# Three-piece weight conversion beside the second and third block pair, and a start with loads on two queues, in a fused attention and two-network kernel

## The chip, the cores and the metric

The kernel runs on one core of a Trainium2 chip. The metric is device time of one execution in microseconds (us). The engines are TensorE (PE, with its weight loads shown as PEld), VectorE (DVE), ScalarE (ACT), GpSimd (POOL) and SyncE (SP); SP computes nothing here, it issues DMAs. ACT issues DMAs too, in line with its arithmetic. "SPq" and "ACTq" in a profile row mark the issue of a DMA.

## The reference

```python
scores = scale * q_c @ k_c.T                # chunks of 64 tokens, 8 heads of 64, batch 8 x 576
attn = exp(scores - max); attn = attn / (sum + 1e-9)
x = (attn @ v_c)                            # 4608 tokens x 512, heads side by side
x = ((x @ moe_w_a) * (x @ moe_w_b)) @ moe_w_out                 # inner width 1536
out = (((x @ w1) * (x @ w2)) @ w3) @ w_out                      # inner width 1024
```

The weights arrive as 64-bit floats and q, k, v as 32-bit floats. The output is 4608 x 512 in 32 bits.

## The kernel before

**Tokens.** The 4608 tokens are nine blocks of 512. Blocks 0 and 1 are done first by plain products, blocks 2 to 7 in three pairs by a seven-product (Strassen) scheme, and block 8 alone; then the second network takes the same blocks. A product works on a high and a low part of each number, three 128x512 matrix instructions for one. One step of a network is one column of 128 inner features (`f`); the first network has 12 steps, the second 8. A pair starts with a burst (the output products of the pair before it) and goes on with its 12 steps.

**Beside the products.** Attention for later blocks is cut into pieces (`turn`, `scores`, `soft2`, `flip`, `apply`) in units of two heads of one block, and the conversion of weights into further pieces. A `Track` hands out pieces at marked points of a step, so that its share of the pieces is out when its share of the points has passed. All engines run what is written to them in the order of writing; nothing is moved at run time.

**Conversion.** The first network's weights are converted at the start, those of the second network beside the second and third pair: 40 tiles of 128x512. A tile is loaded by SP (512 KB, L173). Step one (`s1`) is a bit operation on VectorE (L179) and a rescaling on ScalarE (L180). Step two (`s2`) is three operations on VectorE (L185, L188, L189) and a sum on GpSimd (L195). The result is stored to HBM by ScalarE's queue (L157). `Pump` keeps the order. Its `run` first lets stores go that are due, then calls `begin`, which does `s1` for tiles up to two past the last finished one, then `s2` of the next tile. Beside the pairs a tile has two pieces, `run` and then a load, and there are three places for raw tiles, so the load of tile n+2 takes the place of tile n-1, whose store must have landed.

```python
            self.begin(self.done + 2)
            c, sink, eng = self.jobs[self.done]
            c.s2(eng)
...
            return [p for _ in range(n) for p in ((2.2, False, pump.run), (0.6, False, load))]
```

**Inside a step of a pair.** Four PSUM banks take the products (names `P`, L807). ScalarE copies three of them away (`c`, L892) and VectorE adds to those copies (L895) and multiplies (L922); a bank is free for a later product when its copy or sum is done. Then come pieces at the points, in the same queues.

**Start.** Units 0 to 3 (block 0) are loaded before all else: q, k, v of a unit in turn on SP, three weight tiles on ScalarE's queue. `ask` collects loads and `settle` writes them to a queue. q and k are turned by TensorE (L467) and copied by ScalarE with the tokens put back into order (L468); the softmax is scaled by VectorE (L370). A converted pair of weights gets its high part on ScalarE (L662) and its low part on VectorE (L658). Beside block 0's first three steps (`AHEAD`) run the units 4 to 7 of block 1 and three conversions a step, one in the first.

## Time and profile before

| | before |
|---|---|
| median of 3 runs | 1804.84 us (1803.17 to 1807.74) |
| the profiled execution's own time | 1824.92 us |
| its span, first to last instruction | 1823.1 us |
| mean granted TensorE clock | 0.948 of full |
| TensorE busy | 1625.3 us (89%) |
| VectorE, ScalarE, GpSimd busy | 888.3, 552.9, 449.7 us |

The profiled execution is one run with the hardware profiler on; it is 20.08 us (1.1%) longer than the median of the runs without it. Busy time is the time in which an engine has an instruction in work. A TensorE at clock 1.00 runs at 2.4 GHz, at half of that at 1.2 GHz. The stages of the span are: start and block 0's attention to 43.92 us, blocks 0 and 1 to 281.67, first pair to 517.60 (its steps from 331.85), second pair to 778.74 (steps from 560.28), third pair to 1050.69 (steps from 819.51), block 8 to 1254, second network to the end.

### The profile page before, as it was taken

To read this page: it belongs to the slowest core of one execution; us is meant where nothing else is said; L and a number is where in the kernel's file an instruction comes from. 1 tells how busy PE (TensorE), PEld (TensorE's weight loads), DVE (VectorE), ACT (ScalarE), POOL (GpSimd) and SP (SyncE) were. 2 spreads that over 40 slices of the span, in tenths; PEclk is the share of its full clock that TensorE was granted. 3 is DMA by queue.
4 is the path that set the end of the run, shared out by engine and by line. 5 is a ranking of instruction groups with operands and counts; after the bars stand their busy time and mean duration, and the time that the engine had idled before them with its cause. 6 is when DMAs were issued, how large, how long until landed. Compare 5 with 4: busy or idle time off the path is not lost.

```text
span 1823.1 us, 24483 instructions
## 1 busy us (share of the span) xinstructions
PE 1625.3 (89%) x8968; PEld 1289.9 (71%) x8968; DVE 888.3 (49%) x1460; ACT 552.9 (30%) x989; POOL 449.7 (25%) x350
## 2 busy tenths in 40 slices
PE   5789999889998887897887797999999999999998
PEld 3567777667776665675665676778877877878887
DVE  5658756565763554564455533345234252252231
ACT  4434434222242221242221242223132142242232
POOL 1223323111141221242232240001232231231232
PEclk8789999999999998998898898999999999999999
DMA  8658766776778677586775577878666666676685
GB/s 209 219 172 262 254 202 173 226 215 188 246 223 238 194 199 205 193 249 221 231 228 191 194 256 265 325 296 300 208 225 225 208 222 228 208 231 208 196 280 176
DMA packets 302071, 409.55 MB, mean 225 GB/s; under 512 B 176000, under 2 KB 196480, under 8 KB 301952
## 3 DMA queue, kind: packets, MB, share of 16 engines
q1 hardware_dynamic: 265568, 318.85, 57.9%
q10 hardware_dynamic: 36384, 89.14, 12.8%
q8 instruction: 71, 1.16, 0.3%
q14 instruction: 48, 0.39, 0.1%
HBM read 321.91 MB, written 85.98 MB: 224 GB/s over the span
## 4 chain that ended last, share of the span: by engine, by line
PE 40%; DMA 5%; DVE 2%; issue 2%; POOL 1%; ACT 1%; SPq 0%; ACTq 0%; POOLq 0%; DVEq 0%
PE P L807 22%; PE acc L836 12%; PE wf L1060 3%; DMA cv<-in_moe_w_dram 2%; PE pa0L L793 2%; PE pb0L L793 2%; DMA d<-cv 1%; DMA wo<-dwo 1%; DMA w<-dw 0%; DVE c L895 0%; PE w3p L1050 0%; ACT ev L845 0%; DMA su<-d 0%; DMA x2d<-ev 0%; POOL gl_5b L243 0%
## 5 line engine op out<-in xcount | busy, mean ns | idle before, releaser
L807 PE MATMUL P<-xP,w 128*128 128x512 f32 (+1 forms) x3192 | 777.0, 397 | 102.1 <-DVE c L895 51.2
L807 PEld LDWEIGHTS P<-xP,w 128*128 128x128 f32 x3192 | 597.2, 196 | 249.9 <-DVE c L895 60.8
L895 DVE TENSOR_TENSOR c<-P,c 128x512 f32<-128x512 f32 (+1 forms) x228 | 149.7, 660 | 341.4 <-PE P L807 332.6
L892 ACT COPY c<-P 128x512 f32<-128x512 f32 (+1 forms) x228 | 128.1, 564 | 229.2 <-PE P L807 219.8
L923 POOL TENSOR_TENSOR G<-c,c 128x512 f32<-128x512 f32 x68 | 88.5, 1302 | 416.5 <-DVE c L895 416.2
L242 ACT CAST gh<-c 128x512 fp32r<-128x512 f32 x68 | 42.2, 621 | 356.0 <-DVE c L922 342.1
L836 PE MATMUL acc<-gh,wo 128*128 128x512 f32 x384 | 145.1, 415 | 0.0
L243 POOL TENSOR_TENSOR gl<-c,gh 128x512 fp32r<-128x512 f32 x68 | 90.0, 1324 | 172.7 <-ACT gh L242 172.7
L836 PE MATMUL acc<-wo,gh 128*128 128x512 f32 x320 | 111.3, 391 | 0.5 <-ACT gh L242 0.5
L922 DVE TENSOR_TENSOR c<-P,c 128x512 f32<-128x512 f32 x68 | 46.9, 690 | 129.2 <-PE P L807 129.2
L836 PEld LDWEIGHTS acc<-gh,wo 128*128 128x128 f32 x384 | 76.5, 199 | 17.9
L195 POOL TENSOR_TENSOR cv<-cv 128x512 f32<-128x512 f32 x40 | 46.2, 1155 | 149.6 <-DVE cv L189 118.1
L793 PE MATMUL pa<-xq,w 128*128 128x512 f32 x288 | 78.0, 422 | 1.0 <-ACT xq L242 0.8
L836 PE MATMUL acc<-gl,wo 128*128 128x512 f32 x192 | 78.6, 409 | 0.0
L793 PE MATMUL pb<-xq,w 128*128 128x512 f32 x288 | 72.0, 400 | 0.8 <-DVE G0p L946 0.8
L845 ACT COPY ev<-acc 128x512 f32<-128x512 f32 x72 | 42.3, 588 | 95.2 <-PE acc L836 85.5
L836 PEld LDWEIGHTS acc<-wo,gh 128*128 128x128 f32 x320 | 60.1, 188 | 14.0 <-ACT gh L242 1.0
L793 PEld LDWEIGHTS pa<-xq,w 128*128 128x128 f32 x288 | 57.3, 204 | 14.9 <-ACT xq L242 1.6
L243 DVE TENSOR_TENSOR xP<-xP,xP 128x512 fp32r<-128x512 f32 (+1 forms) x56 | 46.7, 875 | 35.4 <-ACT xP L242 35.4
L836 PE MATMUL acc<-wo,gl 128*128 128x512 f32 x160 | 63.1, 394 | 0.8 <-POOL gl L243 0.8
L793 PEld LDWEIGHTS pb<-xq,w 128*128 128x128 f32 x288 | 54.5, 192 | 12.7 <-DVE G0p L946 1.2
L243 DVE TENSOR_TENSOR xP<-x,xP 128x512 fp32r<-128x512 f32 (+1 forms) x48 | 55.9, 1209 | 2.0 <-ACT xP L242 2.0
(149 smaller groups left out, 2291.8 us busy)
## 6 DMA issues: line engine op xcount, KB each, us to landing
w<-dw SPq DMA_DIRECT2D x228, 512.0 KB, 4.4
wo<-dwo SPq DMA_DIRECT2D x168, 512.0 KB, 4.6
dw<-w ACTq DMA_DIRECT2D x48, 512.0 KB, 5.2
w<-dw SPq DMA_DIRECT2D x92, 256.0 KB, 3.2
d<-cv ACTq DMA_DIRECT2D x40, 256.0 KB, 4.3
su<-d SPq DMA_DIRECT2D x20, 512.0 KB, 5.6
cv_o<-in_moe_w_out_dram SPq DMA_DIRECT2D x18, 512.0 KB, 5.3
x2d<-ev ACTq DMA_DIRECT2D x36, 256.0 KB, 4.7
```

Source lines behind the costliest of these rows:

```text
L195: eng.tensor_tensor(self.w, hi.bitcast(F32), lo, op=ALU.add)
L242: nc.scalar.copy(dst_h, src)
L243: eng_l.tensor_tensor(dst_l, src, dst_h, op=ALU.subtract)
L793: nc.tensor.matmul(ps, w[m][:, kk // 2, wp, kk % 2], xq[kk // 2][:, kk % 2, xp], start=(n == 0), stop=(n == 3 * KM - 1),)
L807: nc.tensor.matmul(ps, w[:, wp, kt], x[:, kt, xp], start=(begins and n == 0), stop=(n == 5), skip_group_check=True,)
L836: nc.tensor.matmul(acc[m], a, b, start=(f == 0 and (wp, gp) == SEQ[0]), stop=(f == NF[ph] - 1 and (wp, gp) == SEQ[-1]),)
L845: nc.scalar.copy(t, acc[m])
L892: nc.scalar.copy(t, src)
L895: add = lambda o, a, b: nc.vector.tensor_tensor(o, a, b, op=ALU.add)
L922: nc.vector.tensor_tensor(g, last, c11, op=ALU.mult)
L923: nc.gpsimd.tensor_tensor(g_place(ph, nm.split("_")[0], f, gplaces), c22, c12, op=ALU.mult)
L1060: nc.tensor.matmul(ps, t[:, gp, jj], wo2[jj // 2][:, jj % 2, wp], start=(jj == 0 and (wp, gp) == SEQ[0]), stop=(jj == NF[1] - 1 and (wp, g ...
```

## The change

Beside the second and third pair a tile now has three pieces: `begin` (`s1` of the next tile), `run` (`s2` of that same tile) and a load; `pump.ahead` is 1 there, so `run` itself begins nothing further. 16 tiles, not 14, go beside the second pair, 24 beside the third.

At the start q and k of four units go to SP first, v of these units to ScalarE's queue behind the three weight tiles. Units 4 and 5 are asked for before the loop, units 6 and 7 within it; the `late` list of pieces, which is not changed, asks for units 6 and 7 as well, so these two are loaded twice (28 DMAs). Two conversions move from the start into block 0's first step. k stays in the order in which TensorE turned it, and the score products read it with a step of 128 elements. In blocks 0 and 1 GpSimd does the softmax scaling, and for five columns the low part of the first weight. The store of a converted tile to `d32` is put into the list of stores when the sum is written, not one tile later.

```diff
--- before.py
+++ after.py
@@ -143,9 +143,9 @@
         asks["left"].append((to, src))
         asks["all"] += 1
 
-    def settle(n):
+    def settle(n, queue=None):
         while asks["done"] < n and asks["left"]:
-            nc.sync.dma_start(*asks["left"].popleft())
+            (queue or nc.sync).dma_start(*asks["left"].popleft())
             asks["done"] += 1
 
     def tick(every=False, loads=0):
@@ -201,7 +201,7 @@
 
         def __init__(self):
             self.jobs, self.done, self.begun, self.loaded = [], 0, 0, 0
-            self.cap, self.last = 0, None
+            self.cap, self.ahead, self.last = 0, 2, None
 
         def add(self, jobs):
             self.jobs.extend(jobs)
@@ -222,7 +222,7 @@
             last, self.last = self.last, None
             if last:
                 last[0]()
-            self.begin(self.done + 2)
+            self.begin(self.done + self.ahead)
             c, sink, eng = self.jobs[self.done]
             c.s2(eng)
             if last:
@@ -260,6 +260,8 @@
         def __init__(self, j, hp, T):
             self.j, self.hp, self.T = j, hp, T
             self.nm = f"{j}_{hp}"
+
+        scaler = nc.vector
 
         def slots(self):
             return dict(tag="qk", bufs=2), dict(tag="v", bufs=2)
@@ -333,17 +335,24 @@
             nc.vector.transpose(self.t[0], self.qb)
             nc.vector.transpose(self.t[1], self.kb)
 
+        def tokens(self, t, r, n):
+
+            return t[r, n * CH : n * CH + CH]
+
         def scores(self):
             qt, kt = self.t
             self.s = self.banks("s")
             for n in range(NCH):
                 m, i = divmod(n, 2)
-                c = slice(n * CH, n * CH + CH)
                 for h in range(2):
                     r = slice(CH * h, CH * h + CH)
                     o = slice(CH * (h ^ i), CH * (h ^ i) + CH)
                     nc.tensor.matmul(
-                        self.s[i][o, m * CH : m * CH + CH], qt[r, c], kt[r, c], start=True, stop=True
+                        self.s[i][o, m * CH : m * CH + CH],
+                        qt[r, n * CH : n * CH + CH],
+                        self.tokens(kt, r, n),
+                        start=True,
+                        stop=True,
                     )
 
         def soft1(self):
@@ -367,7 +376,7 @@
             nc.vector.tensor_reduce(sm, e3, axis=AX.X, op=ALU.add)
             nc.vector.tensor_scalar_add(sm, sm, 1e-9)
             nc.vector.reciprocal(sm, sm)
-            nc.vector.tensor_tensor(
+            self.scaler.tensor_tensor(
                 e3, e3, sm.unsqueeze(2).to_broadcast([P, NCH, CH]), op=ALU.mult
             )
 
@@ -462,13 +471,22 @@
             settle(self.qk_end)
             self.t = [self.work("qT"), self.work("kT")]
             for i, (ps, src) in enumerate(zip(self.banks("t"), (self.qb, self.kb))):
-                for t in range(4):
-                    c = slice(t * P, (t + 1) * P)
-                    nc.tensor.transpose(ps[:, c], src[:, c], ident)
-                nc.scalar.copy(
-                    self.t[i].rearrange("p (i t) -> p t i", t=4),
-                    ps.rearrange("p (t i) -> p t i", t=4),
-                )
+                self.transposed(ps, src)
+                if i:
+                    nc.scalar.copy(self.t[i], ps)
+                else:
+                    nc.scalar.copy(
+                        self.t[i].rearrange("p (i t) -> p t i", t=4),
+                        ps.rearrange("p (t i) -> p t i", t=4),
+                    )
+
+        def transposed(self, ps, src):
+            for t in range(4):
+                c = slice(t * P, (t + 1) * P)
+                nc.tensor.transpose(ps[:, c], src[:, c], ident)
+
+        def tokens(self, t, r, n):
+            return t[r].rearrange("p (t i) -> p i t", t=4)[:, n * CH // 4 : (n + 1) * CH // 4]
 
         def flip_bank(self):
             return psum.tile([P, NT], F32, tag=state["banks"][1], name=f"f_{self.nm}")
@@ -496,11 +514,24 @@
 
 
 
+        scaler = nc.gpsimd
+
         def slots(self):
             n = self.T * NHP + self.hp
-            if n in (2, 3):
-                return dict(tag=f"G{n - 1}"), dict(tag=f"x32_{4 + n}")
+            if n in (2, 3, 4):
+                return dict(tag=f"G{(n - 1) % 3}"), dict(tag=f"x32_{4 + (n + 2) % 4}")
+            if n == 5:
+                return None, dict(tag="x32_7")
             return TurnedOnPE.slots(self)
+
+        def load1(self):
+            if self.slots()[0]:
+                return TurnedOnPE.load1(self)
+            self.qb, self.kb = (
+                pool.tile([P, NT], F32, tag="ev", name=f"qk{self.nm}_{i}", bufs=4) for i in range(2)
+            )
+            self.load_qk()
+            self.qk_end = asks["all"]
 
         def work(self, n):
             i = ["qT", "kT", "e", "pT"].index(n)
@@ -655,10 +686,11 @@
             v2 = w.rearrange("p (o n) -> p o n", o=2)
 
             def low():
-                nc.vector.tensor_tensor(by_part(t, 1), v2, by_part(t, 0), op=ALU.subtract)
+                eng = nc.gpsimd if m == 0 and f < 5 else nc.vector
+                eng.tensor_tensor(by_part(t, 1), v2, by_part(t, 0), op=ALU.subtract)
                 store(dw[0][f][m], whole(t).bitcast(F32))
-                store(d32[0][f][:, m], w)
-
+
+            store(d32[0][f][:, m], w)
             return (lambda: nc.scalar.copy(by_part(t, 0), v2)), low
 
         return [
@@ -1101,12 +1133,15 @@
 
         def later_conv(n):
 
+            pump.ahead = 1
 
             def load():
                 if pump.loaded < pump.done + 2:
                     pump.load(slot(3))
 
-            return [p for _ in range(n) for p in ((2.2, False, pump.run), (0.6, False, load))]
+            begin = lambda: pump.begin(pump.done + 1)
+            one = [(0.5, False, begin), (1.8, False, pump.run), (0.3, False, load)]
+            return one * n
 
         def merged(*lists):
 
@@ -1125,12 +1160,18 @@
 
 
         U = [First(T, hp, T) for T in range(2) for hp in range(NHP)]
-        for i in range(3):
-            pump.load(slot(6), nc.scalar)
         for u in U[:NHP]:
             u.load1()
+            if u.hp == 1:
+                for i in range(3):
+                    pump.load(slot(6), nc.scalar)
+        settle(asks["all"])
+        for u in U[:NHP]:
             u.load2()
-        settle(asks["all"])
+        settle(asks["all"], nc.scalar)
+        for u in U[NHP : NHP + 2]:
+            u.load1()
+            u.load2()
 
         plain = {0: [], 1: []}
         sums = {0: [], 1: []}
@@ -1158,11 +1199,11 @@
                 U[t - 2].flip()
             if 1 <= t < NHP + 1:
                 U[t - 1].soft1()
-            if t in (1, 2):
-                U[t + 3].load1()
-            if t in (3, 4):
-                U[t + 1].load2()
-            if t in (1, 2, 4, 5, 6):
+            if t in (2, 3):
+                U[t + 4].load1()
+            if t in (4, 5):
+                U[t + 2].load2()
+            if t in (1, 2, 6):
                 pump.run()
             if t < 3:
                 pump.load(slot(6), nc.scalar)
@@ -1172,7 +1213,7 @@
         at = None
         for n, (T, f) in enumerate(order):
             if T == 0:
-                conv = Track([conv_piece()] * (1 if f == 0 else 3), 5 if f + 1 < AHEAD else 8)
+                conv = Track([conv_piece()] * 3, 5 if f + 1 < AHEAD else 8)
                 if f + 1 == NF[0]:
                     conv = None
             if T == 1 and f == 0:
@@ -1322,7 +1363,7 @@
                     pump.load(slot(3))
                     pump.load(slot(3))
                 if sb >= 2:
-                    conv = later_conv(14 if sb == 2 else pump.cap - 14 - 3 * NF[0])
+                    conv = later_conv(16 if sb == 2 else pump.cap - 16 - 3 * NF[0])
                     work = merged(work, conv)
                     n_pts = PTS * steps
                 at.append(Track(work, n_pts - 3))
```

VectorE, third pair, step 6 to 7, before: `c` are the copies of products, `cv_n_m` conversion tiles, `mx` and `e` softmax. `s1` (L179) of the next tile stands directly ahead of `s2` of the tile before it.

```order
L895 TENSOR_TENSOR c_6_8330<-P_6_8334,c_6_8330 128x512
L179 TENSOR_SCALAR cv_3_0_8394<-cv_3_0_8394 128x512
L185 SCALAR_TENSOR_TENSOR cv_2_1_8344<-cv_2_1_8344 128x512
L188 TENSOR_SCALAR cv_2_1_8344<-cv_2_1_8344 128x512
L189 SCALAR_TENSOR_TENSOR cv_2_1_8344<-cv_2_1_8344 128x512
L922 TENSOR_TENSOR c_6_8342<-P_6_8334,c_6_8342 128x512
L179 TENSOR_SCALAR cv_3_1_8487<-cv_3_1_8487 128x512
L185 SCALAR_TENSOR_TENSOR cv_3_0_8394<-cv_3_0_8394 128x512
L188 TENSOR_SCALAR cv_3_0_8394<-cv_3_0_8394 128x512
L189 SCALAR_TENSOR_TENSOR cv_3_0_8394<-cv_3_0_8394 128x512
```

The same place now:

```order
L954 TENSOR_TENSOR c_6_8381<-P_6_8374,c_6_8381 128x512
L179 TENSOR_SCALAR cv_3_0_8383<-cv_3_0_8383 128x512
L185 SCALAR_TENSOR_TENSOR cv_3_0_8383<-cv_3_0_8383 128x512
L188 TENSOR_SCALAR cv_3_0_8383<-cv_3_0_8383 128x512
L189 SCALAR_TENSOR_TENSOR cv_3_0_8383<-cv_3_0_8383 128x512
L179 TENSOR_SCALAR cv_3_1_8443<-cv_3_1_8443 128x512
L335 STREAM_TRANSPOSE qT_3_8540<-qk_3_8051 128x512
L336 STREAM_TRANSPOSE kT_3_8541<-qk_3_8051 128x512
L927 TENSOR_TENSOR c_7_8534<-P_7_8544,c_7_8534 128x512
```

L179 of a tile is now followed by L185 of the same tile, here with nothing between for `cv_3_0`; between the two lies ScalarE's L180. Of the 40 tiles 11 have nothing between on VectorE, the others one to nine rows.

SyncE at the start, before: the last loads for units 4 and 5 and the loads of weight tiles 6 to 8, which the second step needs.

```order
L148 DMA v_1_576<-in_v_dram 64x64 x2
L148 DMA v_1_576<-in_v_dram 64x3x64
L148 DMA v_1_576<-in_v_dram 64x4x64
L148 DMA v_1_576<-in_v_dram 64x3x64
L148 DMA v_1_576<-in_v_dram 64x4x64
L173 DMA cv_2_0_694<-in_moe_w_a_dram 128x4x256
L173 DMA cv_2_1_696<-in_moe_w_b_dram 128x4x256
L173 DMA cv_o_698<-in_moe_w_out_dram 128x1024
```

The same place now:

```order
L148 DMA v_2_591<-in_v_dram 64x3x64
L148 DMA v_2_591<-in_v_dram 64x4x64
L148 DMA v_3_635<-in_v_dram 64x64 x2
L148 DMA v_3_635<-in_v_dram 64x3x64
L148 DMA v_3_635<-in_v_dram 64x4x64
L148 DMA v_3_635<-in_v_dram 64x3x64
L148 DMA v_3_635<-in_v_dram 64x4x64
L173 DMA cv_2_0_708<-in_moe_w_a_dram 128x4x256
L148 DMA qk_2_724<-in_q_dram 16x4x64 x2
L173 DMA cv_2_1_756<-in_moe_w_b_dram 128x4x256
L173 DMA cv_o_813<-in_moe_w_out_dram 128x1024
```

Ahead of `cv_2_0` now stand the loads for units 4 to 7, 56 in place of 28, and behind it a second set for unit 6.

ScalarE at the start, before: weight loads, then the first copies.

```order
L173 DMA cv_0_0_250<-in_moe_w_a_dram 128x4x256
L173 DMA cv_0_1_252<-in_moe_w_b_dram 128x4x256
L173 DMA cv_o_254<-in_moe_w_out_dram 128x1024
L468 ACT_TABLE_LOAD
L468 COPY qT_0_288<-t_0_0_290 128x4x128
L468 COPY kT_0_289<-t_0_0_291 128x4x128
```

Now:

```order
L173 DMA cv_0_0_252<-in_moe_w_a_dram 128x4x256
L173 DMA cv_0_1_254<-in_moe_w_b_dram 128x4x256
L173 DMA cv_o_256<-in_moe_w_out_dram 128x1024
L148 DMA v_0_276<-in_v_dram 128x4x64 x2
L148 DMA v_1_277<-in_v_dram 128x4x64 x2
L148 DMA v_2_278<-in_v_dram 128x4x64 x2
L148 DMA v_3_279<-in_v_dram 128x4x64 x2
L478 ACT_TABLE_LOAD
L478 COPY qT_0_293<-t_0_0_295 128x4x128
L476 COPY kT_0_294<-t_0_0_296 128x512
```

Eight loads of v stand ahead of ScalarE's first copies; each of them waits for an earlier load of the start, the last four for the first four.

## Rows read from the trace of the kernel before

**Rows 1.** Windows: stretch, us, busy us (count) of PE, PEld, DVE, ACT, POOL; clock.

```profile
331.85:517.60 185.75, 168.66 (x1118) 130.82 (x1116) 114.11 (x215) 50.14 (x95) 31.40 (x24) 0.96 0.73 220
560.28:778.74 218.46, 180.51 (x1150) 138.75 (x1149) 117.46 (x221) 48.37 (x89) 46.05 (x38) 0.90 0.70 209
819.51:1050.69 231.18, 180.73 (x893) 137.81 (x892) 115.62 (x205) 49.98 (x87) 56.88 (x49) 0.86 0.68 213
```

**Rows 2.** Waits of VectorE in the second pair's steps: us in total, times, longest.

```profile
DVE cv_w L179 <- DMA cv_w<-in_moe_w_dram: 23.0, 5, 10.8
DVE cv_o L179 <- DMA cv_o<-in_moe_w_out_dram: 14.0, 4, 5.4
```

**Rows 3.** Waits of VectorE in the third pair's steps, same columns.

```profile
DVE cv L179 <- DMA cv<-in_moe_w_dram: 37.1, 9, 7.9
DVE cv_w L179 <- DMA cv_w<-in_moe_w_dram: 18.7, 4, 7.6
DVE cv_w L179 <- DMA v<-in_v_dram: 7.8, 1, 7.8
```

**Rows 4.** Timeline, second pair: start, us, engine, line, [idle before, releaser].

```profile
574.35 1.30 SPq L173 DMA_DIRECT2D cv_o<-in_moe_w_out_dram  x1
580.22 0.43 DVE L179 TENSOR_SCALAR cv_o<-cv_o 128x512 int32<-128x512 int32 x1 [5.43 <-DMA cv_o<-in_moe_w_out_dram]
580.68 0.68 ACT L180 ACTIVATE cv_o<-cv_o 128x512 f32<-128x512 f32 x1 [4.75 <-DVE cv_o L179]
581.88 5.49 PE L807 MATMUL P<-xP,w 128*128 128x512 f32 x12 [4.02 <-ACT c L892]
```

**Rows 5.** DMA issues in the third pair's steps: count, KB, median us to landing.

```profile
cv<-in_moe_w_dram SPq DMA_DIRECT2D x16, 512.0 KB, 5.4
d<-cv ACTq DMA_DIRECT2D x16, 256.0 KB, 4.3
```

**Rows 6.** Chain that ended last, second network: start us, us, what.

```profile
1264.56 1.40 PE P L807 x6
1276.96 1.40 PE P L807 x6
```

**Rows 7.** Timeline, second pair: the score products of one attention unit.

```profile
619.72 0.69 PE L345 MATMUL s<-kT,qT 64*64 64x64 f32 x32
```

**Rows 8.** Timeline, VectorE waiting for a ScalarE step that it has just enabled.

```profile
64.69 0.69 DVE L185 SCALAR_TENSOR_TENSOR cv<-cv 128x512 int32<-128x512 int32 x1 [2.87 <-ACT cv L180]
...
338.71 0.69 DVE L243 TENSOR_TENSOR w<-su,w 128x512 fp32r<-128x512 f32 x1 [1.14 <-ACT w L242]
```

**Rows 9.** Timeline of the start: ScalarE's first copy, SyncE's queue, a first conversion step.

```profile
9.98 1.07 ACT L468 COPY qT<-t 128x512 f32<-128x512 f32 x1 [6.40 <-PE t L467]
...
35.36 8.20 SPq L148 DMA_DIRECT2D v<-in_v_dram  x12
43.66 0.55 SPq L173 DMA_DIRECT2D cv<-in_moe_w_a_dram  x1
...
59.98 1.83 DVE L179 TENSOR_SCALAR cv<-cv 128x512 int32<-128x512 int32 x2
```

**Rows 10.** Timeline, first network's third step: a store, the load behind it, TensorE.

```profile
75.76 0.45 ACTq L157 DMA_DIRECT2D d<-cv  x1
...
78.75 0.37 SPq L173 DMA_DIRECT2D cv<-in_moe_w_a_dram  x1
...
89.05 1.08 PE L467 MATMUL t<-ident,qk 128*128 128x128 f32 x4 [1.27 <-DMA qk<-in_k_dram]
```

**Rows 11.** Groups by shape, blocks 0 and 1: count, busy us, mean ns.

```profile
L468 ACT COPY kT<-t 128x512 f32<-128x512 f32 x16 | 17.9, 1120 | 3.1 <-PE t L467 3.1
L483 ACT COPY pT<-f 128x512 f32<-128x512 f32 x16 | 9.3, 584 | 19.1 <-PE f L480 19.0
L195 POOL TENSOR_TENSOR cv<-cv 128x512 f32<-128x512 f32 x24 | 29.5, 1231 | 58.0 <-DVE cv L189 55.8 <-DMA qk<-in_k_dram 1.1 <-DMA v<-in_v_dram 1.1
L370 DVE TENSOR_TENSOR e<-e,sm 128x512 f32<-128x512 f32 x16 | 12.4, 777 | 0.6
```

## The prediction, written before the changed kernel ran

> **What bounds the kernel now.** I read the page first: TensorE is busy for 89% of the span, at a mean clock of 0.948. So time can come from two places: stretches where it idles, and stretches where it runs at less than 1.00. The windows over the steps of the three pairs show both [rows 1]. Each pair has the same 12 steps of products. The first pair, which converts no weights, takes 185.75 us; its TensorE idles 185.75 - 168.66 = 17.1 us at clock 0.96. The second takes 218.46 us, idle 37.95, clock 0.90. The third takes 231.18 us, idle 50.45, clock 0.86, although it has 225 matrix instructions fewer than the first. VectorE is busy for about half of each, so its amount of work is not the limit.
>
> Next I asked what VectorE waits for in the two slow pairs. In both it is L179, the first operation of a conversion tile, waiting for the tile's own load: 23.0 + 14.0 = 37.0 us in the second pair [rows 2], 37.1 + 18.7 + 7.8 = 63.6 us in the third [rows 3], 100.6 together. One such wait, followed through the timeline [rows 4], shows why it reaches TensorE: the load is issued at 574.35, L179 waits 5.43 us and runs at 580.22, ScalarE stands in its rescaling (L180) until 580.68, the copy `c` out of PSUM (L892) is queued behind it, and TensorE idles 4.02 us for that copy. The 12 products after it take 5.49 us: half speed, 1.2 GHz, after a stop. At full speed such a group is quicker, and that is the lower clock of these windows.
>
> The cause is in the order. A tile's pieces cost 2.2 and 0.6; the load of tile n+2 is a piece of 0.6 before the `run` that starts with L179 on that tile. Per tile the second pair has 218.46/14 = 15.6 us, the third 231.18/26 = 8.9, so the load is due 0.6/2.8 of that earlier: 3.3 and 1.9 us. It lands 5.4 us after issue [rows 5]. It is late nearly always.
>
> **The change part by part. Conversion in three pieces.** `s1` now takes the tile that `s2` takes next, so between the load of tile n+2 and its `s1` lie the three pieces of tile n+1: a whole period, about 190/16 = 11.9 us in the second pair and 184/24 = 7.7 us in the third (the lengths are those worked out below). Both are above 5.4. The load also waits for the store of tile n-1, which goes out at the start of `run`, 1.8 of 2.6 parts of a period ahead: 5.3 us in the third pair, and the store takes 4.3 [rows 5]. The margin is thin, 1 us, but a miss only delays SyncE, and the load has 2.3 us in hand there. I take the load waits as gone.
>
> What is left is sized by the first pair, which has the products without the waits [rows 1]. Second pair: 185.75, and with 16 tiles some 122 us of VectorE work for 114.11 (117.46 now; a tile is four operations of 0.43 to 0.69 us [rows 4, 8], two tiles some 4.5). Half of the 8 us more may show: 190, so -28.5. This agrees with the parts: 20.9 us of idle time above the first pair's, and 7.6 of 180.51 us busy for the clock. Third pair: two tiles fewer, and fewer matrix instructions (the scores of a unit take 0.69 us on TensorE [rows 7]; with transposes and the rest I set 6 us for four units): 184, so -47.
>
> **The wait that is added.** L185 now follows L179 of the same tile, with ScalarE's L180 between. On VectorE 11 of 40 tiles have nothing between; elsewhere other rows cover it. Behind a waiting L185 stand VectorE's additions and multiplications of products (L922), for which TensorE waits. The price where ScalarE is free is near the 1.14 us of L243, where it is busy near the 2.87 us of the start [rows 8]. 11 tiles at 1.14 to 2.87 are 12.5 to 31.6 us on VectorE, which has half of its time free; I put a third of the lower, +5 (0 to +28, by 0.88 for TensorE's share as below).
>
> **The start.** Here I find more cost than gain. ScalarE's queue gets eight loads of v ahead of its first copy, now at 9.98 [rows 9]. All eight wait for earlier loads, the last four for the first four; at 5.4 us each turn [rows 5] ScalarE would be free near 14 to 15 us: up to +5.3. SyncE has 28 more loads ahead of the weight tile whose load is issued at 43.66; 12 take 8.20 us, 0.68 each [rows 9], so it goes at about 43.66 + 28 x 0.68 = 62.7, less what SyncE saves on the v loads it gives up; 60.7 taken, landing at 66. L179 of that tile runs at 59.98 now: up to +6. Two conversions fall into block 0's first step (+2). Units 6 and 7 loaded twice cost SyncE the same 0.68 a load, counted in these 28. On the other side VectorE loses four scalings of 0.78 [rows 11] from the start, and the `d32` store listed a tile earlier lets SyncE's next load go sooner: SyncE's load came 3.0 us after the store, and TensorE's turn waited 1.27 us for a k load in that queue [rows 10]. I allow -4 for it over the first steps. Sum of the start: +5, range -4 to +20.
>
> **k not reordered.** ScalarE's copy falls from 1120 to 584 ns [rows 11], 16 times, off the path: at most 8.6 us of ScalarE time. TensorE now reads k with a step of 128 elements. No row shows such a product. From below it costs nothing; from above, if it slows as the strided copy does, 16 units x 0.69 [rows 7] x (1120/584 - 1) = 10.1 us. Most units run beside products, but all of it is TensorE time: I take +2, nearer to nothing since the copy's factor comes with writing by steps too. The Trainium skill speaks against this edit: "Advanced Engine Details and Errata", section "Memory Cachelines", has 16-byte lines in SBUF and a penalty where each access falls on another line, as with a step of 512 bytes. By that page the 10 us end would be the one to take, and the sum 8 us higher; the strided copy's 1120 ns against 584 [rows 11] agrees with it, and no run so far has it on TensorE.
>
> **GpSimd's share.** Sixteen scalings (777 ns on VectorE) and five low parts, at the rate of GpSimd's own 128x512 operation, 1231 ns [rows 11]: 0.45 us longer each, on the way from softmax to the second turn. GpSimd is idle for three quarters of the span, and units run ahead of their use; nothing taken, up to 16 x 0.45 = 7 if it is on the path.
>
> **Sum**, against the profiled execution's own 1824.92: -28.5 - 47 + 5 + 5 + 2 = -63.5, so 1761.4. The median of the runs shown is 0.989 of that execution, so 1742.
>
> **The rivals.** *(a) Deeper.* The first pair is itself not at its floor: a step of the second network, with little beside it, takes 12.40 us [rows 6], 12 of them 148.8. If without late loads both pairs go halfway from the first pair's length to that floor with attention (about 160 and 154), they take some 175 and 169.5: -105, with the other terms -98, so 1708. For it: the first pair still stops for conversions of other kinds that these pairs don't have. Against it: its 17 us of idle time come with PSUM copies, which all pairs have.
>
> *(b) Half.* The store's 1 us margin fails, or the load is held by other DMAs in SyncE's queue (one wait in the third pair is put down to a v load [rows 3]). Then half of the idle 88.4 us goes, 44, and the clock stays; with +12 for the rest -32: 1773.
>
> *(c) The other side.* If ScalarE is never free when `s1` is done, every tile pays on VectorE: 2.87 [rows 8] and one product group of 1.40 [rows 6] while L180 stands behind a copy that waits for it, 4.27 x 40 = 171 us for the 100.6 removed. TensorE idled 88.4 us for those 100.6, a factor 0.88: +62, with the start +69, so 1873. It decides where a tile waits 2.4 us on average: 40 x 2.4 = 96, times 0.88 and the 12 us of other terms eat the gain. For it: the 11 bare tiles. Against it: L180 follows L179 by 0.46 us in the row where it is queued first [rows 4].
>
> *(d) The start eats part.* ScalarE's block, SyncE's 19 us more of issues and the strided read at their upper ends, +20 and +10, with the new wait at 12: net -34 and, where block 0's steps run short of loads as well, -20: 1784 to 1800. The Trainium skill, "DMA: Bandwidth & Descriptors", section "Issuing engines are not separate DMA queues", says that loads from two engines share the same 16 DMA engines and that a second queue saves only issue time. By it the v loads on ScalarE gain no more than their issues; the trace agrees in that SyncE spends 0.68 an issue there [rows 9].
>
> **How the numbers follow.** Forecast 0.60, own range 1722 to 1772; (a) 0.14; (b) 0.14; (c) 0.07, in part or whole; (d) 0.05. From 0.3% (5.4 us) on a measurement of this kernel can be told from no change. The forecast, (a), (b) and most of (d) are faster: 0.88 with what (c) leaves of a small gain taken out; same 0.04; slower 0.08. The range leaves a tenth out at each end: low 1703, a little past (a), high 1800, past (b) to the end of (d).
>
> **What would show it.** In the steps of the second and third pair VectorE's waits at L179 for a DMA should be gone, the windows near 190 and 184 us with clock 0.95 or more, and a new wait of L185 for ScalarE's L180 of 12 to 32 us. ScalarE's first copy should stand near 15 us, the load of `cv_2_0` near 57 to 61, a `d32` store ahead of where it stood. The forecast is wrong if L179 still waits for loads (b), if L185's waits are as long as L179's were (c), or if blocks 0 and 1 end more than 15 us after 281.67 (d). If the score products of blocks 0 and 1 take 1.3 us a unit, the strided read costs.

## The result, and the profile after

| | before | after |
|---|---|---|
| median of 4 runs each, on one chip | 1806.29 us | 1751.14 us (1744.5 to 1759.31) |
| ratio, 95% interval | 1 | 0.9697 (0.965 to 0.9744) |
| the profiled execution's own time | 1824.92 us | 1759.31 us |
| VectorE's waits for raw tiles at L179, pairs two and three | 100.6 us | 23.6 us |
| start of the first burst | 281.67 us | 287.03 us |

The kernel is 3.0% faster; 1742 with a range of 1703 to 1800 was forecast. Of the lines read here some have moved: L807 is now L839, L892 is L924, L895 is L927, L922 is L954, L396 is L405, L345 is L350, L468 is L476 and L478, L483 is L501, L370 is L379.

First the windows of the changed kernel, with the columns of [rows 1] (the two numbers behind the clock are the share of the DMA engines that is busy and GB/s): start, blocks 0 and 1, and the steps of the three pairs.

```profile
0.00:45.20 45.20, 18.74 (x304) 14.92 (x305) 16.65 (x43) 15.99 (x27) 8.16 (x13) 0.90 0.89 204
45.20:287.03 241.83, 215.16 (x1624) 171.19 (x1620) 165.36 (x282) 99.92 (x177) 82.29 (x67) 0.93 0.71 219
339.72:526.30 186.58, 168.22 (x1118) 129.93 (x1116) 113.90 (x215) 50.12 (x95) 31.49 (x24) 0.96 0.73 218
567.20:772.99 205.79, 175.01 (x1150) 136.27 (x1148) 125.46 (x229) 49.10 (x90) 48.93 (x40) 0.93 0.76 229
813.89:984.08 170.19, 159.09 (x893) 125.58 (x892) 118.15 (x201) 49.23 (x86) 57.08 (x48) 0.97 0.86 280
```

Set beside [rows 1], the third pair lost 61.0 us (231.18 to 170.19), at clock 0.97 for 0.86; the second lost 12.7 (218.46 to 205.79), at 0.93 for 0.90; the first stayed as it was. Blocks 0 and 1 begin 3.8 us later than before (45.20 for 41.44, which is the first product of block 0; the 43.92 named ahead is its second group) and end 5.4 later; the burst behind them takes 2.5 us more. So -73.7 in the two pairs, some +8 at the start, and the rest of the program within 2 us. Of the 61.0 us in the third pair 39.4 are idle time of TensorE (50.45 to 11.10) and 21.6 busy time (180.73 to 159.09) at the higher clock; in the second pair it is 7.2 and 5.5.

VectorE's waits in the second pair (us in total, times, longest) answer to [rows 2]:

```profile
DVE cv_w L179 <- DMA cv_w<-in_moe_w_dram: 17.1, 5, 6.5
DVE cv_o L185 <- ACT cv_o L180: 13.6, 1, 13.6
DVE cv_o L179 <- DMA cv_o<-in_moe_w_out_dram: 1.6, 1, 1.6
```

and those in the third pair to [rows 3]:

```profile
DVE cv_w L185 <- ACT cv_w L180: 18.0, 5, 13.1
DVE cv L185 <- ACT cv L180: 6.3, 7, 1.5
DVE cv L179 <- DMA cv<-in_moe_w_dram: 4.9, 3, 3.6
```

These load waits went from 63.6 to 4.9 us in the third pair, from 37.0 to 18.7 in the second. The new wait of L185 for L180 is there. Its longest, 13.6 and 13.1 us, stand at each window's edge, where ScalarE's queue is still in the burst; [rows 2] left out the like of it, 15.8 us before the change. Without these two it is 4.9 + 6.3 = 11.2 us.

Why the second pair still waits is seen on its timeline: the store that frees a place, L179 of the tile before, SyncE's issues ahead of the raw tile, and VectorE's wait for it.

```profile
645.88 0.33 ACTq L157 DMA_DIRECT2D do<-cv_o  x1
...
664.58 1.54 DVE L179 TENSOR_SCALAR cv_w<-cv_w 128x512 int32<-128x512 int32 x1
...
668.94 0.37 SPq L745 DMA_DIRECT2D w<-dw  x1
669.36 2.69 SPq L148 DMA_DIRECT2D qk<-in_k_dram  x4
672.15 0.42 SPq L745 DMA_DIRECT2D w<-dw  x1
672.62 0.90 SPq L148 DMA_DIRECT2D qk<-in_k_dram  x2
673.61 0.37 SPq L173 DMA_DIRECT2D cv_w<-in_moe_w_dram  x1
...
679.04 0.43 DVE L179 TENSOR_SCALAR cv_w<-cv_w 128x512 int32<-128x512 int32 x1 [3.59 <-DMA cv_w<-in_moe_w_dram]
```

The raw tile (`cv_w`) is issued at 673.61 behind loads of k and w, and L179 runs at 679.04, 5.43 us later, after 3.59 us of waiting. In the list of pieces this load stands ahead of L179 of the tile before it, which ran at 664.58; SyncE gets to it 9 us after that. The place had long been free, since the store of three tiles earlier went out at 645.88 and took 2.5 us to land. It is so in the whole pair: the loads go out 5.8 to 28 us after the landing of the store that frees their place, where in the third pair 8 of 21 go within 0.1 us of it. The attention pieces for the next pair load q, k and v through the same queue, 152 DMAs in this window.

### The profile page after: what moved, and what is told of

The parts are those of the page before. It is cut to its first block, busy times and chain, and to the rows that moved or that the text cites. A ratio compares the mean times of both kernels' runs of the same rounds, so it can differ in the third digit from the quotient of the medians.

```text
span 1757.5 us, 24550 instructions
## 1 busy us (share of the span) xinstructions
PE 1600.5 (91%) x8968; PEld 1278.5 (73%) x8968; DVE 892.8 (51%) x1447; ACT 546.9 (31%) x989; POOL 465.5 (26%) x363
## 4 chain that ended last, share of the span: by engine, by line
PE 67%; DMA 14%; DVE 8%; issue 3%; SPq 3%; ACT 2%; POOL 1%; ACTq 0%; POOLq 0%; DVEq 0%
PE P L839 31%; PE acc L868 20%; PE pa L825 3%; PE pb L825 3%; SPq L148 3%; PE wf L1092 3%; DMA wo<-dwo 3%; PE pa0L L825 2%; DVE c L927 2%; PE pb0L L825 2%; DMA v<-in_v_dram 1%; DMA qk<-in_q_dram 1%; PE x L405 1%; DMA qk<-in_k_dram 1%; DMA cv_w<-in_moe_w_dram 1%
## 5 line engine op out<-in xcount | busy, mean ns | idle before, releaser
L839 PE MATMUL P<-xP,w 128*128 128x512 f32 (+1 forms) x3192 | 750.7, 388 | 50.9 <-DVE c L927 33.0
L839 PEld LDWEIGHTS P<-xP,w 128*128 128x128 f32 x3192 | 583.0, 191 | 187.6 <-DVE c L927 42.0
L927 DVE TENSOR_TENSOR c<-P,c 128x512 f32<-128x512 f32 (+1 forms) x228 | 149.9, 661 | 302.9 <-PE P L839 293.0
L924 ACT COPY c<-P 128x512 f32<-128x512 f32 (+1 forms) x228 | 128.3, 564 | 213.6 <-PE P L839 209.9
L954 DVE TENSOR_TENSOR c<-P,c 128x512 f32<-128x512 f32 x68 | 47.0, 691 | 129.1 <-PE P L839 129.0
L825 PEld LDWEIGHTS pa<-xq,w 128*128 128x128 f32 x288 | 57.0, 202 | 13.5 <-issue 0.9
L825 PEld LDWEIGHTS pb<-xq,w 128*128 128x128 f32 x288 | 53.3, 188 | 12.5 <-DVE G0p L978 1.2
L243 POOL TENSOR_TENSOR gl0L<-sa0L,gh0L 128x512 fp32r<-128x512 f32 x12 | 16.0, 1334 | 160.6 <-ACT gh0L L242 160.6
```

What stands on the lines that cost most here:

```text
L243: eng_l.tensor_tensor(dst_l, src, dst_h, op=ALU.subtract)
L825: nc.tensor.matmul(ps, w[m][:, kk // 2, wp, kk % 2], xq[kk // 2][:, kk % 2, xp], start=(n == 0), stop=(n == 3 * KM - 1),)
L839: nc.tensor.matmul(ps, w[:, wp, kt], x[:, kt, xp], start=(begins and n == 0), stop=(n == 5), skip_group_check=True,)
L924: nc.scalar.copy(t, src)
L927: add = lambda o, a, b: nc.vector.tensor_tensor(o, a, b, op=ALU.add)
L954: nc.vector.tensor_tensor(g, last, c11, op=ALU.mult)
```

## Experiments

All ratios are to the kernel before on the same chip. Each profile is one execution; the start of the first burst came between 280.2 and 285.3 us in seven profiles of kernels with the old start, so single differences of some 3 us there are not read as effects. The steps of the pairs vary as well: in six profiled kernels with the same code for pairs two and three (the changed kernel, `conv_only`, `k_reordered`, `v_on_sync`, `loaded_once`, `all_fixed`) pair two takes 202 to 209 us, pair three 167 to 172, both together 371 to 379.

**The three pieces alone, and the start alone.** `conv_only` is the kernel before with the conversion part of the diff:

```diff
-            return [p for _ in range(n) for p in ((2.2, False, pump.run), (0.6, False, load))]
+            begin = lambda: pump.begin(pump.done + 1)
+            one = [(0.5, False, begin), (1.8, False, pump.run), (0.3, False, load)]
+            return one * n
```

with `pump.ahead = 1` and the split 16/24. `start_only` is the changed kernel with these lines and the split turned back.

> The kernel before with the three conversion pieces and the split 16/24 alone; the start is the old one. Theory one (the load's distance to L179 is the gain, the start costs 8 us): steps of pair two near 206 us and of pair three near 170 as in the changed kernel, block 0 to the first burst as before (281.7), in all 8 us below the changed kernel: ratio to before 0.961 to 0.967. Rival (the start's edits hold up part of the gain, since VectorE is relieved there): no better than the changed kernel, ratio 0.970 or above.

> The changed kernel with the old two pieces per tile and the old split 14/26: only the start's edits are left. Theory one: the pairs as before (218 and 231 us), the first burst at 287 in place of 281.7, ratio 1.002 to 1.007. Rival: the start gains by itself, ratio below 0.998.

`conv_only`: 1746.74 us, 0.9657 (0.9619 to 0.9695). `start_only`: 1816.25 us, 1.0052 (1.0029 to 1.0075). Windows of the steps of pairs two and three, `conv_only`:

```profile
558.87:762.25 203.38, 175.50 (x1150) 135.46 (x1149) 125.32 (x229) 48.90 (x90) 48.60 (x40) 0.93 0.76 232
803.40:971.85 168.45, 157.20 (x894) 123.91 (x893) 117.95 (x201) 49.08 (x86) 57.19 (x48) 0.98 0.88 283
```

and `start_only`:

```profile
565.31:777.11 211.80, 175.63 (x1149) 135.13 (x1148) 117.68 (x221) 48.41 (x89) 46.11 (x38) 0.93 0.73 215
816.99:1044.04 227.05, 177.94 (x894) 136.03 (x893) 115.50 (x205) 49.97 (x87) 56.92 (x49) 0.89 0.69 217
```

The whole gain is in the conversion part; the start costs 0.3 to 0.75%, 5 to 14 us. `start_only` shows something else as well. Its pairs are ordered as before the change, and take 211.80 + 227.05 = 438.85 us, where the profile before has 449.64. The execution that the prediction was reckoned from was a long one, by 10.8 us in just these windows: 3.1 idle and 7.7 busy time of TensorE, at clock 0.90 and 0.86 where `start_only` has 0.93 and 0.89. `start_only`'s own first burst begins at 284.44, inside the spread above, so that its profile does not show in which stage its 5 to 14 us are lost. Against 438.85 the changed kernel's 375.98 is a gain of 62.9, not 73.7.

**Distance or separation?** Two things changed for a tile at once: its load is a full period ahead of L179, and its `s1` has become a piece of its own. `back_to_back` keeps two pieces and the split 14/26 and changes only the distance, at the price that L185 stands straight behind L179 in all 40 tiles:

```diff
-            self.begin(self.done + 2)
+            self.begin(self.done + self.ahead)
...
         def later_conv(n):
+            pump.ahead = 1
```

> The kernel before with run beginning only the tile that it finishes, still two pieces and 14/26: L179 and L185 of a tile stand in one piece for all 40 tiles, the load is two pieces (one period) ahead. Theory one (distance of the load): load waits at L179 fall from 100.6 us to under 30, L185 waits for L180 in nearly every tile at 1 to 3 us, some 60 us on VectorE, of which half shows: 1765 to 1785 us, ratio 0.978 to 0.989. Rival (the third piece, which puts other work between L179 and L185, is what gains): no gain, ratio 0.995 or above.

1749.57 us, 0.9688 (0.9655 to 0.9721): the expectation was too cautious by some 15 us. Its windows:

```profile
564.98:764.21 199.23, 174.83 (x1150) 135.40 (x1148) 117.64 (x221) 47.58 (x88) 45.51 (x38) 0.93 0.75 228
805.06:981.89 176.83, 160.65 (x893) 123.98 (x892) 123.65 (x211) 49.81 (x88) 58.56 (x50) 0.98 0.86 279
```

and VectorE's waits at L185, the first two rows in pair two, the others in pair three, and behind them the largest load wait that is left:

```profile
DVE cv_o L185 <- ACT cv_o L180: 24.5, 8, 16.2
DVE cv_w L185 <- ACT cv_w L180: 6.3, 6, 1.6
DVE cv_w L185 <- ACT cv_w L180: 23.4, 10, 14.5
DVE cv L185 <- ACT cv L180: 16.4, 16, 2.4
DVE cv L179 <- DMA cv<-in_moe_w_dram: 1.8, 3, 1.3
```

Two pairs in 376.06 us, as in the changed kernel (375.98). Without the longest of each pair (16.2 and 14.5, at the edge of the window as above) the L185 waits are 39.9 us in 38 tiles, 1.05 each. The same tiles in three pieces (`conv_14`, below) take 377.07 us, so the waits of all 40 tiles cost the two pairs nothing that can be seen. A load's distance of one period is enough for the gain, without the third piece; rival (c), which priced such a wait at 4.27 us on TensorE's path, is refuted at its own point.

**The split.** `conv_14` is `conv_only` with 14/26.

```diff
-conv = later_conv(16 if sb == 2 else pump.cap - 16 - 3 * NF[0])
+conv = later_conv(14 if sb == 2 else pump.cap - 14 - 3 * NF[0])
```

> As conv_only, but 14 tiles beside pair two and 26 beside pair three. Theory one (each tile costs what its late load and its waits cost, and pair two's loads are the later ones, behind the loads for attention on SyncE): pair two shorter by 4 to 8 us, pair three longer by 4 to 10, in all within 5 us of conv_only. Rival (the split is a large part of the gain): 10 us or more above conv_only.

1750.46 us, 0.9688 (0.9654 to 0.9721). Its windows, and VectorE's load wait at L179 in pair two:

```profile
559.31:757.20 197.89, 171.32 (x1150) 133.57 (x1148) 118.21 (x221) 48.12 (x88) 46.56 (x38) 0.91 0.78 230
798.07:977.25 179.18, 162.48 (x893) 125.89 (x892) 124.28 (x211) 50.07 (x88) 59.34 (x50) 0.96 0.85 275
DVE cv_w L179 <- DMA cv_w<-in_moe_w_dram: 1.7, 1, 1.7
```

Pair two is 5.5 us shorter and pair three 10.7 longer than in `conv_only`. The sum is 5 us longer in the profile and 4 in the medians; the intervals overlap, and which split is better is not resolved. With 14 tiles and the same 152 loads of q, k and v the load waits of pair two are all but gone: a period of 197.89/14 = 14.1 us was enough there, one of 203.38/16 = 12.7 was not.

**What holds pair two.** Two candidates: SyncE's queue, or the store that frees the place. `load_on_gpsimd` loads the raw tiles of `conv_only` from GpSimd's queue; `early_store` issues the store one piece (`begin`) earlier.

```diff
# load_on_gpsimd
-                    pump.load(slot(3))
+                    pump.load(slot(3), nc.gpsimd)
# early_store
-            begin = lambda: pump.begin(pump.done + 1)
+            begin = lambda: (tick(True), pump.begin(pump.done + 1))
```

> As conv_only, with the raw tiles beside pairs two and three loaded from GpSimd's queue. Theory one (what is left in pair two, 203 us, is raw tiles issued late behind attention's loads on SyncE): the 23 us of load waits at L179 in pair two under 8, pair two at 192 to 198 us; pair three unchanged or worse by what GpSimd loses waiting for the store that frees a place (up to 5 us a tile); ratio 0.960 to 0.966. Rival (the store of the place is what is late): the load waits stay above 15 us and GpSimd's own work is delayed, ratio above 0.967.

> As conv_only, with the store of the tile before issued at begin in place of run, 0.5 of 2.6 parts of a period earlier (2 to 2.5 us). Rival of the last run as theory: if the store holds the load, load waits at L179 in pair two fall from 23 us to under 15, ratio 0.961 to 0.965. If SyncE's queue holds it, they stay at 18 or more and the time is that of conv_only within 4 us.

`load_on_gpsimd`: 1748.82 us, 0.968 (0.963 to 0.9731), with these windows:

```profile
554.77:752.86 198.09, 170.66 (x1150) 132.96 (x1148) 124.54 (x229) 49.20 (x90) 57.69 (x56) 0.93 0.79 238
793.34:975.24 181.90, 163.06 (x894) 127.31 (x892) 122.04 (x201) 49.09 (x86) 71.93 (x70) 0.95 0.81 262
```

In pair two no load wait at L179 is left (18.4 + 4.8 us in `conv_only`), and the pair takes 198.09 us for 203.38. Pair three takes 181.90 for 168.45, where GpSimd now waits for the store of the place (its waits there):

```profile
POOL cv L173 <- DMA d<-cv: 14.1, 5, 3.9
POOL cv_w L173 <- DMA dw<-cv_w: 5.3, 2, 3.9
```

Issuing costs GpSimd too: the 22 loads there take 12.7 + 3.5 = 16.2 us of its time (0.59 to 0.79 each). How much of the 13.5 us belongs to either was not run. The ratio misses the 0.960 to 0.966 of theory one because of pair three.

`early_store`: 1753.71 us, 0.9688 (0.9643 to 0.9733). VectorE's main load wait in pair two is then

```profile
DVE cv_w L179 <- DMA cv_w<-in_moe_w_dram: 13.0, 4, 5.4
```

for 18.4 us in `conv_only` (with the `cv_o` tiles 16.7 for 23.2), and the pair takes 205.83 us: inconclusive between its two outcomes, no gain. Its stores go out only 1.4 us earlier on average. With the landings read from the trace above it is clear all the same: in pair two SyncE's queue holds the load; in pair three the store does, and SyncE, which has 28 loads of q, k and v there and not 152, is the engine that can wait for it at less cost.

**The start, edit by edit.** `k_reordered` puts k back into order, `v_on_sync` puts the first eight v loads back on SyncE behind their q and k (and the three weight tiles first on ScalarE's queue), `loaded_once` drops the second load of units 6 and 7, `all_fixed` does all three.

```diff
# k_reordered
-                if i:
-                    nc.scalar.copy(self.t[i], ps)
...
-        def tokens(self, t, r, n):
-            return t[r].rearrange("p (t i) -> p i t", t=4)[:, n * CH // 4 : (n + 1) * CH // 4]
# v_on_sync
         for u in U[:NHP]:
             u.load1()
...
+            u.load2()
...
-        for u in U[:NHP]:
-            u.load2()
-        settle(asks["all"], nc.scalar)
# loaded_once
-        late = Track(attention_pieces(U[NHP:]), 5 * AHEAD)
+        late = Track(attention_pieces(U[NHP:], False), 5 * AHEAD)
...
-            if i + 2 < len(ps):
+            if loads and i + 2 < len(ps):
```

> The changed kernel with ScalarE putting k's tokens back into order and the score products reading it without a step. Theory one (the strided read costs TensorE, seen as 1.11 us a unit for 0.69): score products of blocks 0 and 1 back to 0.69 us at full clock, 13.1 us busy in place of 18.5, ScalarE's copy back to 1120 ns; 3 to 6 us below the changed kernel, ratio to before near 0.966. Rival (that TensorE time lies in waits anyway): no change of the first burst's start at 287.

> The changed kernel with the eight first v loads back on SyncE, unit by unit behind q and k, and the three weight tiles first on ScalarE's queue. Theory one (the loads block ScalarE): first ScalarE copy back from 17.1 to about 10 us, block 0's products begin near 41.5 in place of 45.2; 2 to 5 us below the changed kernel, unless SyncE's longer queue takes it back. Rival (SyncE's queue with 28 loads more is what costs): products begin earlier but the first burst stays near 287.

> The changed kernel without the second load of units 6 and 7 (28 DMAs fewer on SyncE, behind the weight tiles of the second step and among those of later steps). Theory one (the second load costs SyncE 0.68 us a DMA, 19 us of its queue, while TensorE waits for other things): blocks 0 and 1 shorter by 0 to 4 us, ratio to before 0.966 to 0.970. Rival (SyncE's queue is what costs at the start): 6 us or more shorter, first burst near 281.

> The changed kernel with k reordered, v on SyncE and units 6 and 7 loaded once; units 4 to 7 still loaded early, softmax scaling of blocks 0 and 1 and five low parts on GpSimd, the earlier d32 store. Theory one (these three edits hold all of the start's cost): block 0's products at 40 to 41, first burst at 275 to 282, ratio 0.961 to 0.966, at or below conv_only. Rival (what GpSimd took over costs too): first burst at 284 or later, ratio above 0.966.

| kernel | median us | ratio (interval) | blocks 0 and 1 begin | first burst begins |
|---|---|---|---|---|
| changed kernel | 1751.14 | 0.9697 (0.965 to 0.9744) | 45.20 | 287.03 |
| `k_reordered` | 1748.07 | 0.9671 (0.9625 to 0.9716) | 46.25 | 282.07 |
| `v_on_sync` | 1752.59 | 0.9692 (0.9645 to 0.9739) | 40.06 | 286.64 |
| `loaded_once` | 1752.25 | 0.9694 (0.9663 to 0.9724) | 45.86 | 282.16 |
| `all_fixed` | 1750.58 | 0.9693 (0.9657 to 0.9729) | 39.44 | 283.26 |

No total can be told from that of the changed kernel. Nor are the starts of the first burst more than a hint, since `start_only`, with the changed kernel's start, has 284.44. `all_fixed` misses its theory one (275 to 282, at most 0.966), which speaks against the three edits holding all of the start's cost; its interval overlaps that of `conv_only`. What can be read are busy times and waits. Groups in blocks 0 and 1 of the changed kernel (score products, k's copy, the scaling on GpSimd):

```profile
L350 PE MATMUL s<-kT,qT 64*64 64x64 f32 x512 | 18.5, 290 | 9.4 <-ACT kT L476 8.2 <-DVE xq L243 0.7 <-ACT x L419 0.5
L476 ACT COPY kT<-t 128x512 f32<-128x512 f32 x16 | 10.2, 640 | 0.0
L379 POOL TENSOR_TENSOR e<-e,sm 128x512 f32<-128x512 f32 x8 | 8.5, 1067 | 11.2 <-DVE sm L378 6.1 <-ACT xq L242 3.3 <-ACT qT L478 1.0
```

and of `k_reordered`:

```profile
L350 PE MATMUL s<-kT,qT 64*64 64x64 f32 x512 | 13.0, 241 | 10.3 <-ACT kT L475 9.1 <-DVE xq L243 0.7 <-ACT x L419 0.5
L475 ACT COPY kT<-t 128x512 f32<-128x512 f32 x16 | 17.9, 1120 | 2.2 <-PE t L483 2.2
```

512 score products take 18.5 us with the step of 128 elements and 13.0 without, on TensorE itself, 16 x 0.34 us; ScalarE's copy is 0.48 us shorter for it. One unit in the changed kernel, beside the 0.69 us of [rows 7], both at a granted clock of 1.00:

```profile
188.96 1.11 PE L350 MATMUL s<-kT,qT 64*64 64x64 f32 x32
```

The third row of the groups shows a miscount of the prediction: 8 scalings went to GpSimd, not 16, at 1067 ns.

The start of the changed kernel (timeline), first ScalarE's queue, then the weight tile that the second step needs:

```profile
4.95 10.86 ACTq L148 DMA_DIRECT2D v<-in_v_dram  x8
15.84 1.28 ACT L478 ACT_TABLE_LOAD   x1 [15.84 <-DMA v<-in_v_dram]
17.13 1.05 ACT L478 COPY qT<-t 128x512 f32<-128x512 f32 x1
18.67 1.16 PE L350 MATMUL s<-kT,qT 64*64 64x64 f32 x32 [7.45 <-ACT kT L476]
...
61.05 0.42 SPq L173 DMA_DIRECT2D cv<-in_moe_w_a_dram  x1
67.67 0.43 DVE L179 TENSOR_SCALAR cv<-cv 128x512 int32<-128x512 int32 x1 [6.58 <-DMA cv<-in_moe_w_a_dram]
68.13 0.67 ACT L180 ACTIVATE cv<-cv 128x512 f32<-128x512 f32 x1 [5.64 <-DVE cv L179]
68.70 0.57 ACT L501 COPY pT<-f 128x512 f32<-128x512 f32 x1
69.33 1.23 PE L405 MATMUL x<-pT,v 64*64 64x64 f32 x32 [5.86 <-ACT pT L501]
```

Eight v loads hold ScalarE from 4.95 to 15.81; the first copy stands at 17.13 (9.98 in [rows 9]), and TensorE waits 7.45 us for the k copy. The weight tile's load is issued at 61.05 (43.66), L179 waits for it 6.58 us, L180 and behind it `pT` stand, and TensorE waits 5.86. In `v_on_sync`:

```profile
10.01 1.07 ACT L478 COPY qT<-t 128x512 f32<-128x512 f32 x1 [6.41 <-PE t L486]
...
69.66 0.43 DVE L179 TENSOR_SCALAR cv<-cv 128x512 int32<-128x512 int32 x1 [13.93 <-DMA cv<-in_moe_w_a_dram]
71.32 1.13 PE L405 MATMUL x<-pT,v 64*64 64x64 f32 x32 [13.21 <-ACT pT L501]
```

The first copy is back at 10.01, and all of it is lost at the second place: L179 now waits 13.93 us for the same tile, TensorE 13.21. The load stands behind 56 loads for units 4 to 7 on SyncE in both kernels, and moving the v loads there adds to the queue. `all_fixed` keeps these 56 ahead, and L179 waits 12.67 us there. So L179's wait for that tile, issued behind these 56 loads, sets block 0's second step, not ScalarE's block. That the loads themselves are the cause is argued: asking for units 6 and 7 behind the weight tile was not run, nor were the two conversions moved into block 0's first step or GpSimd's share put back alone, which `all_fixed` keeps as well.

**The better version.** `gpsimd_pair_two` is `conv_only` with GpSimd's queue for the raw tiles beside pair two and SyncE's beside pair three; `fixed_and_gpsimd` is `all_fixed` with the same choice of queues.

```diff
+        def later_conv(n, queue=None):
...
-                    pump.load(slot(3))
+                    pump.load(slot(3), queue)
...
-                    conv = later_conv(16 if sb == 2 else pump.cap - 16 - 3 * NF[0])
+                    conv = later_conv(16 if sb == 2 else pump.cap - 16 - 3 * NF[0], nc.gpsimd if sb == 2 else None)
```

> conv_only with the raw tiles loaded from GpSimd's queue beside pair two alone, from SyncE's beside pair three. Both theories are told apart by the sum: pair two at 198 as with GpSimd's queue in both, pair three at 168 to 170 as in conv_only, ratio 0.962 to 0.965; if pair three still is near 180, what pair two does with its queue is handed on, ratio 0.967 or above.

> The last two together: the sum of both gains against conv_only if they are independent, ratio 0.957 to 0.963; 0.964 or above if one of them is taken back.

`gpsimd_pair_two`: 1737.83 us, 0.9617 (0.9586 to 0.9648), steps of pairs two and three:

```profile
562.04:758.74 196.70, 169.20 (x1150) 131.88 (x1148) 124.47 (x229) 49.19 (x90) 57.57 (x56) 0.95 0.80 240
798.88:969.76 170.88, 159.29 (x894) 125.53 (x892) 117.67 (x201) 49.00 (x86) 57.05 (x48) 0.97 0.87 279
```

196.70 and 170.88: pair two is as short as with GpSimd's queue in both, pair three is within the 167 to 172 of SyncE's. It has the lowest median here; its interval ends just below that of the changed kernel but overlaps that of `conv_only`, so the total is not resolved from the latter. `fixed_and_gpsimd` came to 1741.29 us, 0.9642 (0.9608 to 0.9675), 198.82 and 168.19 in the pairs: the changed start, even mended in three places, brings nothing to it, and the 0.957 to 0.963 expected of the sum of both was missed.

What VectorE waits for in pair two of `gpsimd_pair_two` is now attention's own k:

```profile
DVE kT L334 <- DMA qk<-in_k_dram: 20.6, 4, 7.1
```

`conv_only` has 15.2 us in this row, the changed kernel 9.0. These loads, still on SyncE, are a candidate for what to bring forward next; this was not run.

## Why the prediction held, and where it was off

**The mechanism was right.** A raw tile loaded too near its first use stalls VectorE, ScalarE's queue behind it and TensorE behind that; `back_to_back` shows that the distance alone removes it. Two sizes in it were off by more than 10 us and in opposite directions, so that the closeness of the sum is in part luck. The 100.6 us also leave out two rows of the same kind, where L179's wait is put down to another DMA: 3.9 us in the second pair (a q load) and 6.8 in the third (a `w` load).

**Third pair, -47 forecast, -61.0 measured** (-56.9 against `start_only`'s 227.05). The first pair was taken as its measure, less 6 us for four attention units. It is 16.4 us longer than the third now is: 9.1 of that is TensorE's busy time, where 6 was set, and 7.3 its idle time (18.4 for 11.1). The first pair has waits of its own that the third lacks: VectorE there waits 17.4 us to turn k of attention (9.8 put down to k loads, 7.6 to v loads), which the third pair, with half the units, does not show. That these make the idle time is argued, not shown. Rival (a) had this direction with 169.5, and 170.19 came.

**Second pair, -28.5 forecast, -12.7 measured** (-6.0 against `start_only`'s 211.80). The step that failed is "a whole period between the load of tile n+2 and its `s1`". That is the distance in the list of pieces, but SyncE issued in the order written, and with q, k and v loads for attention ahead of it the load went out 5.43 us ahead of L179 in the row above. Rival (b) named this queue, and was right for the second pair. The waits left there were 18.7 us. They are about half of the miss: without them pair two takes 196.70 to 198.82 us in three profiles with 16 tiles, still 7 to 9 above the 190 forecast, so the first pair's length with half of "the 8 us more" was too short a measure as well. What holds those 7 to 9 us stays open; TensorE idles 27.5 us in `gpsimd_pair_two`'s 196.70 for the first pair's 17.1. The two misses nearly cancel: -73.7 for -75.5.

**The added wait, +5.** 11.2 us on VectorE for 12.5 to 31.6 forecast. What it costs TensorE was not resolved; `back_to_back`, with waits in nearly all tiles, puts it below what the spread of the pairs can tell.

**The start, +5 (and +2 for k), some +8 measured** in the profile, 5 to 14 by `start_only`. ScalarE's first copy at 17.13, not 14 to 15; the weight tile's load at 61.05 for 60.7, L179 at 67.67 for a landing at 66, TensorE's stall 5.86 for "up to +6". The gain of 4 for the earlier `d32` store was not measured by itself. k's strided read cost +5.4 us of TensorE time for the +2 taken, within the bounds of 0 and 10.1; 1.11 us a unit, for the 1.3 named as the mark. The Trainium skill, "Advanced Engine Details and Errata", section "Memory Cachelines", says that accesses pay a penalty when each falls on another line of 16 bytes. The trace agrees in sign for this step of 512 bytes, with a factor of 1.6 (1.11/0.69), where the strided copy's ratio was 1.9. The Trainium skill, "DMA: Bandwidth & Descriptors", section "Issuing engines are not separate DMA queues", says that another issuing engine saves only issue time. The trace differs in what that is worth: in pair two issuing the raw tiles on GpSimd made the pair 5 us shorter (203.38 to 198.09), as it was the place in SyncE's queue that was late.

**The total.** -65.6 us from profile to profile for -63.5 forecast, but -55 from median to median. The changed kernel's profiled execution is 0.5% above its median (1759.31 for 1751.14), not the 1.1% taken by the scaling with 0.989: the extra of the long profile, 10.8 us in these two pairs, was counted into the gain. That is most of the 9 us between 1742 and 1751.

## What to carry to other kernels

Count the distance between a load and its first use in what the issuing engine has to do in between, not in the list that the work is cut from: a full period of 7 us was enough in the third pair (170.19/24), and one of 12.7 us not in the second, where the same queue carried 152 loads of q, k and v. A wait of one engine for another within a tile (1 us) is cheap beside a late load (100.6 us in 23 waits before, 4.4 us each, and a stopped TensorE), so the load's lead is bought first. When a stall in the start is mended, look at the next row that waits: the 7 us that ScalarE's first copy gained in `v_on_sync` came back whole as a later tile's wait.

## What was not expected of the hardware

Units of 64x64 products take 1.6 times as long when k is read with a step of 128 32-bit elements: 32 of them take 1.11 us for 0.69. And a load issued by GpSimd stopped GpSimd while its place was not free: 14.1 + 5.3 us of such waits and 16.2 us of issuing stand in its queue in pair three, between the sums that it makes for TensorE's operands, and the pair took 13.5 us longer than with SyncE issuing.
